# A fused linear attention and feed-forward kernel: token chunks of 512 instead of 384, with the buffers and PSUM banks shared out anew

## The chip, the cores and the metric

The kernel runs on one core of a Trainium2 chip. The metric is the device time of one launch in microseconds (us). A core has TensorE (PE in the profile; its weight loads are PEld), VectorE (DVE), ScalarE (ACT), GpSimd (POOL) and SyncE (SP), which here issues every DMA. PSUM, where PE writes its sums, has eight banks; one bank holds 512 float32 values in each of the 128 partitions.

## The reference

```python
kv  = np.einsum('bhsd,bhse->bhde', k, v)          # 8 batches, 8 heads, 576 positions, 64 wide
out = np.einsum('bhsd,bhde->bhse', q, kv)
rms = np.sqrt(np.mean(out * out, axis=-1, keepdims=True) + 1e-06)
x   = out / rms * g_norm                          # rearranged to 4608 tokens x 512
h   = x @ w_in                                    # 512 x 2048
g   = h * np.cos(h)
y   = g @ w_out                                   # 2048 x 512
```

The two weight matrices come as float64, and the tokens of all batches stand one behind the other.

## The kernel before, in words

The 4608 tokens are cut into 12 chunks of 384 (`CH`). For a chunk, the d_ff dimension of 2048 is walked in 16 blocks of 128 (`j`). One chunk with one block is a *step*, so there are 192 steps. Every float32 operand of a large product is held as a high and a low part, and a product is three matmuls (high x high, low x high, high x low).

A step has these parts. **Stage 1** (`stage1_part`) makes h for the block: for each of 4 slices `p` of the 512 features a triple of matmuls 384 columns wide, 12 in all, into one PSUM bank `ps_h` (three of them, tokens `t_h`). **The elementwise chain** (`act_part`) is, in order: `ki` on ACT (h over 2 pi, rounded), two DVE instructions that reduce h to `r`, sine and square on ACT (half the angle: cos h = 1 - 2 sin² (h/2)), a DVE product with h, which is the last reader of the bank and gives it back, then `ghi` on ACT and `glo` on DVE. **Stage 2** (`stage2_part`) multiplies g by the block of w_out: for each tile of 128 tokens a triple of matmuls 512 columns wide into a bank `acc` that sums over all of d_ff (three tiles and three banks, 9 matmuls). The two banks left, `ps_a`, serve the attention.

Attention for a chunk is done beside the steps of the chunk ahead of it: `kv_part` makes k^T v of a pair of heads, `x_part` turns q into x for one slice `p` (transposes on DVE, the product with kv, the norm with a power on POOL) and writes `xhi` and `xlo`, of which a chunk's tiles are held in a pool of two. The first two chunks (`FRONT`) take another path: PE transposes q and the products are plain float32. `w_part` turns each 128-row block of float64 weights into a high and a low float32 part, with about three instructions on ACT and three on DVE, 512 wide; 32 such halves (16 of w_in, 16 of w_out) are made. So that not all are needed at once, the first steps run as: chunk 0 with blocks 0 to 7, chunk 1 with blocks 0 to 7, chunk 0 with 8 to 15, chunk 1 with 8 to 15, then chunk by chunk. The partial sums of chunks 0 and 1 go to DRAM in between.

The order of instructions on PE, ACT, DVE and POOL is fixed ahead of time by a planner in the kernel (`Order`). Each part is a generator that waits for events, takes tokens (one for each buffer) and asks for time on an engine with a priority; `due(i)` gives the priorities of step `i`. The durations in these requests are written by hand, and the planner's own times decide nothing but the order. SP works through its DMAs in order. At the end `out_part` copies each `acc` bank to SBUF on ACT (buffers `ob`, two of them; the last tile of the last chunk goes into a spare `kt` buffer) and stores it.

```python
    t_x, t_wst, t_h, t_ki, t_r, t_g, t_osb = Tokens(2), Tokens(3), Tokens(3), Tokens(2), Tokens(3), Tokens(3), Tokens(2)
    def due(i):
        return 20.0 + 4.0 * i
    segments = [(0, 0, 8), (1, 0, 8), (0, 8, 16), (1, 8, 16)]
```

Of the kernel before, what the change touches and what calls it, by code (L numbers as in the profile page):

```python
# [19 lines left out]
P = 128  # L20
# [125 lines left out]
def tile_kernel(  # L146
# [16 lines left out]
    CH = 384  # L163
# [19 lines left out]
    ps_h = ctx.enter_context(tc.tile_pool(name="ps_h", bufs=3, space=bass.MemoryType.PSUM))  # L183
# [16 lines left out]
    def copiers(on_act, on_dve):  # L200
        return [("ACT", on_act, 0.0), ("DVE", on_dve, 0.3)]
# [45 lines left out]

    def due(i):
        return 20.0 + 4.0 * i
# [22 lines left out]
    x_slot = [Event() for _ in range(NCH)]  # L272
# [3 lines left out]
    t_kv, t_q, t_qT, t_qhl = Tokens(2), Tokens(2), Tokens(1), Tokens(2)  # L276
    t_s1, t_s2, t_psa = Tokens(4), Tokens(1), Tokens(2)
    t_x, t_wst, t_h, t_ki, t_r, t_g, t_osb = Tokens(2), Tokens(3), Tokens(3), Tokens(2), Tokens(3), Tokens(3), Tokens(2)
# [93 lines left out]
    def kv_part(b, p, prio):  # L372
        yield "wait", [kv_in[b, p]] + ([q_used[c, p] for c in chunks_of(b - 2)] if b > 1 else [])
        yield "take", t_psa, prio
        _, end = yield "run", [("PE", 0.95 if b >= FRONT else 1.1)], prio if b < FRONT else -1.0
# [14 lines left out]
        else:  # L390
            e, end = yield "run", copiers(0.21, 0.27), prio
# [6 lines left out]
        yield "run", [("ACT", 0.21)], prio  # L398
# [6 lines left out]
        _, end = yield "run", [("DVE", 0.27)], prio  # L405
# [9 lines left out]
    def kv_split_part(b, p, prio):  # L415

        yield "wait", [kv_done[b, p]]
        yield "run", [("ACT", 0.18)], prio
# [8 lines left out]
    def x_tiles(c):  # L427
        yield "take", t_x
        _, _ = yield "run", [("NONE", 0.0)], -1.0
        xs[c] = (  # L430
            xpool.tile([P, NP, CH], F32R, name="xhi"),
            xpool.tile([P, NP, CH], F32R, name="xlo"),
        )
        sched.fire(x_slot[c], sched.busy["NONE"])
# [6 lines left out]
    def x_part(c, p, prio):  # L441
        yield "wait", [q_in[c, p], x_slot[c]]
        front = c < FRONT
        yield "take", t_qhl, prio
        if front:
            bank = t_psa if c else t_h
            yield "take", bank, prio
            _, _ = yield "run", [("PE", 0.4)], prio
# [6 lines left out]
        else:  # L455
            yield "take", t_qT
            _, end = yield "run", [("DVE", 0.47)], prio
# [3 lines left out]
        if front:  # L461
            e, end = yield "run", copiers(0.41, 0.47), prio
            qT = at.tile([P, CH], F32, name="qhi")
            copy(e, qT, ps_t[:, 0:CH])
            sched.give(bank, end)
        else:
            yield "run", [("ACT", 0.41)], prio
            qhi = at.tile([P, CH], F32R, name="qhi")
            qlo = at.tile([P, CH], F32R, name="qlo")
# [6 lines left out]
        bank = t_acc[p] if c == 0 and p < NTT else t_psa  # L476
        yield "take", bank, prio
        _, end = yield "run", [("PE", 0.5 if front else 0.5 if len(parts) == 1 else 0.7)], prio if front else -1.0
# [12 lines left out]
        sched.give(t_qhl, end)  # L491
        yield "take", t_s1, prio
        yield "run", [("ACT", 0.37)], prio
        sq = at.tile([P, CH], F32, name="s1", bufs=4)
        act.activation(out=sq, in_=ps[:, 0:CH], func=AF.Square, scale=0.125)
        if front:
            t_xn = t_r if c == 0 and p < NTT else t_s1
            yield "take", t_xn, prio
            _, end = yield "run", [("ACT", 0.46)], prio
            x = ew.tile([P, CH], F32, name="r") if t_xn is t_r else at.tile([P, CH], F32, name="s1", bufs=4)  # L500
            act.activation(out=x, in_=ps[:, 0:CH], func=AF.Copy, scale=gcol)
            _, end = yield "run", [("PE", 0.6)], prio
            sums = ps[:, CH:CH + 2 * NTT]
# [3 lines left out]
            yield "run", [("DVE", 0.13)], prio  # L507
            ms = small.tile([P, 2 * NTT], F32, name="ms")
            dve.tensor_scalar(out=ms, in0=sums, scalar1=EPS, scalar2=None, op0=ALU.add)
            yield "run", [("POOL", 1.2)], prio  # L510
            rinv = small.tile([P, 2 * NTT], F32, name="rinv")
            pool.tensor_tensor(out=rinv, in0=ms, in1=mhalf[:, 0:2 * NTT], op=ALU.pow)
            yield "run", [("ACT", 0.41)], prio
# [10 lines left out]
            sched.give(bank, end)  # L524
        else:
            t_xn = t_s1
            yield "take", t_s2
            yield "run", [("DVE", 0.47)], prio
            sqT = at.tile([P, TB, 32], F32, name="s2", bufs=1)
            dve.transpose(out=sqT.rearrange("p a b -> p (a b)"), in_=sq)  # L530
# [289 lines left out]
```

## Time and profile before

| what | value |
|---|---|
| time, median of 3 runs | 912.48 us (912.03 to 914.66) |
| the profiled execution | 911.69 us, of which the traced span is 909.9 us |
| PE busy | 892.2 us, 98% |
| PE weight loads | 797.2 us, 88% |
| DVE busy | 629.2 us, 69% |
| ACT busy | 553.5 us, 61% |
| POOL busy | 107.6 us, 12% |
| HBM read and written | 46.66 MB and 11.01 MB |

The span is what the trace shows of the program; 1.8 us of the execution's time lie outside it. PE's busy time counts a matmul from its start to its modelled end, and neighbours overlap, so that a PE shown as full can still be waiting a little. What matters for PE is the distance from one matmul's start to the next. The trace has phases: up to about 80 us the DMA engines are full and the weights are made, up to about 150 us the other half of the weights is made, and from then on the steps repeat.

### The profile page before, as it was taken

The page shows a single profiled execution, that of the slowest core. Times are in us where ns is not written, and L with a number is a line of the kernel's source. Part 1 is how long each engine was busy: PE and PEld are TensorE (multiplying, and loading weights), DVE is VectorE, ACT ScalarE, POOL GpSimd, SP SyncE. Part 2 cuts the span into 40 slices and gives each one's busy share as a digit, 9 for nine tenths or more (in the row PEclk, how much of TensorE's full clock was granted, in tenths as well). Part 3 has the DMA queues.
Part 4 walks back from the last instruction along what each step waited for, and adds up shares of the span by engine and source line. Part 5 has one row for each costly group of instructions (what it writes and reads, how often), then busy time and mean ns, then how long its engine had stood idle before and what let it go on. Part 6 is the DMA issues. An engine that isn't in the chain of part 4 may idle for free.

```text
span 909.9 us, 13803 instructions
## 1 busy us (share of the span) xinstructions
PE 892.2 (98%) x5008; PEld 797.2 (88%) x5008; DVE 629.2 (69%) x1276; ACT 553.5 (61%) x1283; POOL 107.6 (12%) x61
## 2 busy tenths in 40 slices
PE   8799998999999999999999999999999999999998
PEld 6787887898899998898889998898889999899997
DVE  3779889877767767767766766776766776766553
ACT  4888887655556555556556656655555665655554
POOL 2120000220101100002000101110110110210000
PEclk9999999999999999999999999999999999999999
DMA  9998010723201003212212002211200110100000
GB/s 247 257 316 282 21 58 2 182 61 88 64 9 52 11 15 91 44 35 70 62 35 53 10 9 79 62 36 52 61 11 10 44 18 9 45 1 1 35 1 35
DMA packets 112244, 58.58 MB, mean 64 GB/s; under 512 B 80432, under 2 KB 103984, under 8 KB 112176
## 3 DMA queue, kind: packets, MB, share of 16 engines
q1 hardware_dynamic: 112176, 57.70, 23.8%
q8 instruction: 39, 0.64, 0.3%
q14 instruction: 29, 0.24, 0.1%
HBM read 46.66 MB, written 11.01 MB: 63 GB/s over the span
## 4 chain that ended last, share of the span: by engine, by line
PE 90%; DMA 3%; DVE 3%; SPq 1%; ACT 1%; issue 1%; POOL 0%; ACTq 0%; DVEq 0%
PE acc L196 43%; PE ps_h L196 42%; PE ps_a L196 5%; DMA wo<-in_moe_w_out_dram 1%; DMA wi<-in_moe_w_in_dram 1%; DVE r L196 1%; DVE sg L196 1%; DMA out_dram<-ob 1%; DMA wo<-in_v_dram 1%; SPq L324 1%; SPq L367 0%; DVE wi L196 0%; DVE glo L196 0%; POOL rinv L196 0%; ACT ki L196 0%
## 5 line engine op out<-in xcount | busy, mean ns | idle before, releaser
L196 PE MATMUL ps_h<-xhi,wi 128*128 128x384 f32 x1536 | 397.1, 339 | 5.6 <-DVE r L196 3.6
L196 PE MATMUL acc<-wo,ghi 128*128 128x512 f32 x1152 | 360.6, 394 | 2.6 <-ACT ghi L196 1.9
L196 PEld LDWEIGHTS ps_h<-xhi,wi 128*128 128x128 f32 x1536 | 281.2, 189 | 22.5 <-DVE r L196 4.8
L196 PE MATMUL ps_h<-xlo,wi 128*128 128x384 f32 x768 | 259.4, 338 | 0.0
L196 ACT ACTIVATE r<-r 128x384 f32<-128x384 f32 x384 | 200.4, 524 | 81.5 <-DVE r L196 76.6
L196 PEld LDWEIGHTS acc<-wo,ghi 128*128 128x128 f32 x1152 | 211.8, 188 | 38.8 <-ACT ghi L196 2.6
L196 PE MATMUL acc<-wo,glo 128*128 128x512 f32 x576 | 227.2, 394 | 0.1
L196 POOL TENSOR_TENSOR rinv<-ms,mhalf 128x12 f32<-128x12 f32 (+1 forms) x48 | 104.8, 2183 | 711.8 <-DVE ms L196 710.6
L196 ACT ACTIVATE ki<-ps_h 128x384 int32<-128x384 f32 x192 | 94.2, 491 | 140.6 <-PE ps_h L196 139.8
L196 DVE SCALAR_TENSOR_TENSOR r<-ki,ps_h 128x384 f32<-128x384 int32 x192 | 105.8, 552 | 87.7 <-ACT ki L196 84.8
L196 DVE SCALAR_TENSOR_TENSOR r<-r,ps_h 128x384 f32<-128x384 f32 x192 | 105.4, 550 | 60.0 <-ACT r L196 59.4
L196 PEld LDWEIGHTS ps_h<-xlo,wi 128*128 128x128 f32 x768 | 144.6, 188 | 0.0
L196 PEld LDWEIGHTS acc<-wo,glo 128*128 128x128 f32 x576 | 108.0, 187 | 24.4 <-DVE glo L196 0.8
L196 DVE TENSOR_TENSOR glo<-r,ghi 128x384 fp32r<-128x384 f32 x192 | 105.7, 551 | 23.9 <-ACT ghi L196 22.3
L196 DVE SCALAR_TENSOR_TENSOR r<-ki,r 128x384 f32<-128x384 int32 x192 | 105.9, 552 | 2.3
L196 ACT CAST ghi<-r 128x384 fp32r<-128x384 f32 x192 | 97.5, 509 | 16.2 <-DVE r L196 14.7
L196 DVE STREAM_TRANSPOSE s<-s 128x384 f32<-128x384 f32 x40 | 23.1, 578 | 41.0 <-ACT s L196 40.7
L196 ACT ACTIVATE s<-ps_a 128x384 f32<-128x384 f32 x45 | 22.1, 491 | 47.1 <-PE ps_a L196 46.9
L196 ACT COPY swp<-part 32x12 f32<-32x12 f32 x160 | 31.7, 198 | 15.8 <-DVE part L196 13.9
L196 DVE STREAM_TRANSPOSE s<-rinv 128x384 f32<-128x384 f32 x40 | 23.0, 575 | 11.2 <-POOL rinv L196 11.1
L196 ACT CAST xhi<-s 128x384 fp32r<-128x384 f32 x45 | 23.0, 511 | 12.1 <-DVE s L196 11.7
L196 DVE TENSOR_TENSOR xlo<-s,xhi 128x384 fp32r<-128x384 f32 x45 | 25.0, 555 | 6.8 <-ACT xhi L196 4.9
(97 smaller groups left out, 517.0 us busy)
## 6 DMA issues: line engine op xcount, KB each, us to landing
out_dram<-ob SPq DMA_DIRECT2D x35, 256.0 KB, 2.1
wi<-in_moe_w_in_dram SPq DMA_DIRECT2D x16, 512.0 KB, 8.5
wo<-in_moe_w_out_dram SPq DMA_DIRECT2D x16, 512.0 KB, 9.1
kt<-in_k_dram SPq DMA_DIRECT2D x24, 256.0 KB, 2.9
vt<-in_v_dram SPq DMA_DIRECT2D x24, 256.0 KB, 3.2
qb<-in_q_dram SPq DMA_DIRECT2D x112, 48.0 KB, 2.3
qb<-in_q_dram SPq DMA_DIRECT2D x96, 24.0 KB, 1.9
part<-ob SPq DMA_DIRECT2D x6, 256.0 KB, 2.0
```

Of the source, the lines that this page charges most:

```text
L196: return lambda *a, **kw: tc.keep_in_program_order(f(*a, **kw))
L324: nc.sync.dma_start(out=t, in_=src[b, 2 * p:2 * p + 2].rearrange("h (p i) d -> p h i d", p=SF))
```

## The change

Chunks are 512 tokens, so there are 9 chunks and 144 steps. A step has 12 matmuls of 512 columns in stage 1 and four tiles, again 12 matmuls, in stage 2. Four banks now hold `acc`, two hold `ps_h`, two `ps_a`. Elementwise instructions are 512 wide. For space, the weight staging shares its buffers (`m`, `sg`, three of each) with the high and low part of q, `ki` has one buffer instead of two, and x is held by slice: six tiles of each kind, four for a chunk and two for the next. Chunk 0 keeps its slices 2 and 3 in the `kt` and `vt` buffers, which are thus taken until step 23; the loads of k and v for batch 2 and later wait for that. The written-in durations and priorities follow (`STEP` is 5.4).

```diff
-    CH = 384
+    CH = 512
-    xpool = ctx.enter_context(tc.tile_pool(name="xpool", bufs=2))
-    wst = ctx.enter_context(tc.tile_pool(name="wst", bufs=3))
+    xpool = ctx.enter_context(tc.tile_pool(name="xpool", bufs=6))
-    at = ctx.enter_context(tc.tile_pool(name="at", bufs=2))
+    at = ctx.enter_context(tc.tile_pool(name="at", bufs=3))
-    ps_h = ctx.enter_context(tc.tile_pool(name="ps_h", bufs=3, space=bass.MemoryType.PSUM))
+    ps_h = ctx.enter_context(tc.tile_pool(name="ps_h", bufs=2, space=bass.MemoryType.PSUM))
+    STEP = 5.4
     def due(i):
-        return 20.0 + 4.0 * i
+        return 20.0 + STEP * i
-    t_s1, t_s2, t_psa = Tokens(4), Tokens(1), Tokens(2)
-    t_x, t_wst, t_h, t_ki, t_r, t_g, t_osb = Tokens(2), Tokens(3), Tokens(3), Tokens(2), Tokens(3), Tokens(3), Tokens(2)
+    t_kv, t_q, t_qT, t_two = Tokens(2), Tokens(2), Tokens(1), Tokens(3)
+    t_s1, t_psa = Tokens(3), Tokens(2)
+    t_x, t_h, t_ki, t_r, t_g, t_osb = Tokens(6), Tokens(2), Tokens(1), Tokens(3), Tokens(3), Tokens(2)
+    def x_tokens(c, p):
+        return t_kv if c == 0 and p >= 2 else t_x
...
-                    out=h, lhsT=w[:, s, cols], rhs=x[:, p, :],
+                    out=h, lhsT=w[:, s, cols], rhs=x,
+            if last_step[c] == i:
+                sched.give(x_tokens(c, p), end)
...
-        prio = due(i + 2) - 4.0
+        prio = due(i + 2) - STEP
-        ki = ew.tile([P, CH], I32, name="ki", bufs=2)
+        ki = ew.tile([P, CH], I32, name="ki", bufs=1)
...
-        first, n = window(chunks_of(b)[0] - 1)
+        first, n = window(chunks_of(b)[0])
-            load(2.1, due(i) - 6.0, [kv_in[b, p]], kv_loads(b, p), take=t_kv)
+            load(2.1, due(i) - 6.0, [kv_in[b, p]], kv_loads(b, p),
+                 wait=[x_done[0, 2], x_done[0, 3]], take=t_kv)
```

Three places in the instruction order follow; tiles have their number behind the name. The first is PE in the steady part, before: the end of one h, a stage 2 of three tiles, and the start of the next h.

```order
L196 MATMUL ps_h_5283<-xhi_3769,wi14_1610 128x384 x2
L196 MATMUL ps_h_5283<-xlo_3770,wi14_1610 128x384
L196 MATMUL acc0_4710<-wo12_1613,ghi_5299 128x512 x2
L196 MATMUL acc0_4710<-wo12_1613,glo_5300 128x512
L196 MATMUL acc1_4717<-wo12_1613,ghi_5299 128x512 x2
L196 MATMUL acc1_4717<-wo12_1613,glo_5300 128x512
L196 MATMUL acc2_4761<-wo12_1613,ghi_5299 128x512 x2
L196 MATMUL acc2_4761<-wo12_1613,glo_5300 128x512
L196 MATMUL ps_h_5283<-xhi_3769,wi14_1610 128x384 x2
L196 MATMUL ps_h_5283<-xlo_3770,wi14_1610 128x384
L196 MATMUL ps_h_5332<-xhi_3769,wi15_1669 128x384 x2
L196 MATMUL ps_h_5332<-xlo_3770,wi15_1669 128x384
```

The same in the changed kernel: the last triple of one h, a stage 2 of four tiles, the first triple of the next h.

```order
L195 MATMUL ps_h_4509<-xhi_4172,wi5_676 128x512 x2
L195 MATMUL ps_h_4509<-xlo_4173,wi5_676 128x512
L195 MATMUL acc0_4352<-wo4_915,ghi_4536 128x512 x2
L195 MATMUL acc0_4352<-wo4_915,glo_4537 128x512
L195 MATMUL acc1_4364<-wo4_915,ghi_4536 128x512 x2
L195 MATMUL acc1_4364<-wo4_915,glo_4537 128x512
L195 MATMUL acc2_4369<-wo4_915,ghi_4536 128x512 x2
L195 MATMUL acc2_4369<-wo4_915,glo_4537 128x512
L195 MATMUL acc3_4375<-wo4_915,ghi_4536 128x512 x2
L195 MATMUL acc3_4375<-wo4_915,glo_4537 128x512
L195 MATMUL ps_h_4582<-xhi_3534,wi6_825 128x512 x2
L195 MATMUL ps_h_4582<-xlo_3535,wi6_825 128x512
```

With two banks, h of step i + 2 goes into the bank of h of step i. Between the end of the one and the start of the other stand, in nearly every step of the changed kernel, the four triples of step i + 1 and four triples of one stage 2. Before, a bank came back three steps later.

The second place is SP's queue where k and v of batch 2 are loaded for the first time, before: among the weight loads.

```order
L367 DMA wi12_795<-in_moe_w_in_dram 128x4x128
L336 DMA qb_944<-in_q_dram 32x12x32 x4
L336 DMA qb_961<-in_q_dram 32x12x32 x4
L313 DMA kt_985<-in_k_dram 128x2x256
L367 DMA wo10_818<-in_moe_w_out_dram 128x512
L313 DMA vt_986<-in_v_dram 128x2x256
L367 DMA wi13_832<-in_moe_w_in_dram 128x4x128
```

And in the changed kernel:

```order
L742 DMA part1_3_1348_1642<-ob_1635 128x512
L723 DMA ob_1944<-part0_0_1000_1158 128x512
L723 DMA ob_2038<-part0_1_1012_1172 128x512
L321 DMA kt_1840<-in_k_dram 128x2x256
L321 DMA vt_1841<-in_v_dram 128x2x256
L321 DMA kt_1866<-in_k_dram 128x2x256
L321 DMA vt_1867<-in_v_dram 128x2x256
L321 DMA kt_1899<-in_k_dram 128x2x256
L321 DMA vt_1900<-in_v_dram 128x2x256
```

The loads moved behind all weights and behind the partial sums, and each waits for the buffer in which chunk 0 kept its slices. On PE, between the last use of the first such buffer (slice 2 of step 23) and the first kv product stand one triple of step 23, two of step 24 and three of a stage 2.

The third place is the end of ACT's queue, before:

```order
L196 CAST ghi_9604<-r_9573 128x384
L196 ACTIVATE r_9607<-r_9607 128x384 x2
L196 CAST ghi_9632<-r_9607 128x384
L196 ACTIVATE ob_9645<-acc0_9144 128x512
L196 ACTIVATE ob_9651<-acc1_9150 128x512
L196 ACTIVATE kt_9653<-acc2_9177 128x512
```

And in the changed kernel:

```order
L195 ACTIVATE r_8154<-r_8154 128x512 x2
L195 CAST ghi_8178<-r_8154 128x512
L195 ACTIVATE ob_8188<-acc0_7653 128x512
L195 ACTIVATE ob_8193<-acc1_7658 128x512
L195 ACTIVATE kt_8200<-acc3_7667 128x512
L195 ACTIVATE ob_8203<-acc2_7662 128x512
```

There is a fourth tile to store; its copy comes last, and uses an `ob` buffer that the first tile's store must have left.

## Rows read from the trace of the kernel before

**Rows 1.** The page's busy times of PE, DVE and ACT over the span.

```profile
PE 892.2 (98%) x5008; PEld 797.2 (88%) x5008; DVE 629.2 (69%) x1276; ACT 553.5 (61%) x1283; POOL 107.6 (12%) x61
```

**Rows 2.** The chain that ended last, shares of the span by line.

```profile
PE acc L196 43%; PE ps_h L196 42%; PE ps_a L196 5%; DMA wo<-in_moe_w_out_dram 1%; DMA wi<-in_moe_w_in_dram 1%; DVE r L196 1%; DVE sg L196 1%; DMA out_dram<-ob 1%; DMA wo<-in_v_dram 1%; SPq L324 1%; SPq L367 0%; DVE wi L196 0%; DVE glo L196 0%; POOL rinv L196 0%; ACT ki L196 0%
```

**Rows 3.** Windows: PE, PEld, DVE, ACT, POOL busy (count), granted clock, DMA share, GB/s.

```profile
40.00:77.00 37.00, 32.43 (x207) 28.10 (x207) 32.27 (x64) 33.30 (x75) 6.29 (x4) 0.95 0.98 299
77.00:112.60 35.60, 35.55 (x177) 32.10 (x178) 30.91 (x62) 29.02 (x61) 0.00 (x0) 1.00 0.37 125
112.60:148.30 35.70, 32.63 (x160) 28.27 (x159) 30.75 (x57) 28.74 (x58) 0.00 (x0) 1.00 0.12 37
200.00:880.00 680.00, 679.16 (x3733) 612.04 (x3732) 461.31 (x943) 393.87 (x928) 82.61 (x36) 1.00 0.15 38
```

**Rows 4.** Instructions grouped by form, up to 76.9 us: count, busy us, mean ns.

```profile
L196 PE MATMUL ps_h<-xhi,wi 128*128 128x384 f32 x64 | 19.7, 388 | 2.3 <-DVE r L196 1.7 <-DVE wi L196 0.6
...
L196 PE MATMUL acc<-wo,ghi 128*128 128x512 f32 x30 | 9.9, 412 | 0.4 <-ACT ghi L196 0.4
```

**Rows 5.** The same groups up to 112.6 us.

```profile
L196 PE MATMUL ps_h<-xhi,wi 128*128 128x384 f32 x128 | 36.1, 363 | 3.8 <-DVE r L196 3.3 <-DVE wi L196 0.6
L196 PE MATMUL acc<-wo,ghi 128*128 128x512 f32 x84 | 26.7, 399 | 0.4 <-ACT ghi L196 0.4
```

**Rows 6.** The same groups up to 148.3 us.

```profile
L196 PE MATMUL ps_h<-xhi,wi 128*128 128x384 f32 x192 | 52.8, 355 | 5.2 <-DVE r L196 3.3 <-ACT wi L196 1.1 <-DVE wi L196 0.8
L196 PE MATMUL acc<-wo,ghi 128*128 128x512 f32 x126 | 39.9, 398 | 1.9 <-ACT ghi L196 1.9
```

**Rows 7.** The last links of the chain in order of time: start us, us.

```profile
891.84 2.10 PE ps_h L196 x12
893.94 2.08 PE acc L196 x9
...
898.13 8.22 PE acc L196 x36
...
906.37 0.60 ACT kt L196
```

**Rows 8.** Elementwise groups by form over the whole span, 384 and 512 wide.

```profile
L196 ACT ACTIVATE r<-r 128x384 f32<-128x384 f32 x384 | 200.4, 524 | 81.5 <-DVE r L196 76.6
...
L196 DVE SCALAR_TENSOR_TENSOR r<-r,ps_h 128x384 f32<-128x384 f32 x192 | 105.4, 550 | 60.0 <-ACT r L196 59.4
...
L196 ACT ACTIVATE ki<-ps_h 128x384 int32<-128x384 f32 x192 | 94.2, 491 | 140.6 <-PE ps_h L196 139.8
...
L196 DVE SCALAR_TENSOR_TENSOR sg<-sg,m 128x512 int32<-128x512 int32 x32 | 21.9, 686 | 2.7 <-ACT m L196 2.1 <-ACT sg L196 0.6
L196 ACT ACTIVATE ob<-acc 128x512 f32<-128x512 f32 x35 | 20.9, 596 | 9.1 <-PE acc L196 4.7 <-DMA out_dram<-ob 4.0
```

**Rows 9.** Timeline of ACT and DVE after an h that ended at 893.94 us.

```profile
893.98 0.49 ACT L196 ACTIVATE ki<-ps_h 128x384 int32<-128x384 f32 x1 [1.05 <-PE ps_h L196]
...
894.50 0.56 DVE L196 SCALAR_TENSOR_TENSOR r<-ki,ps_h 128x384 f32<-128x384 int32 x1 [0.99 <-ACT ki L196]
...
894.98 0.55 DVE L196 TENSOR_TENSOR glo<-r,ghi 128x384 fp32r<-128x384 f32 x1
...
895.45 0.55 DVE L196 SCALAR_TENSOR_TENSOR r<-ki,r 128x384 f32<-128x384 int32 x1
...
897.14 0.55 DVE L196 SCALAR_TENSOR_TENSOR r<-r,ps_h 128x384 f32<-128x384 f32 x1 [1.15 <-ACT r L196]
```

**Rows 10.** Waits from 200 to 880 us: PE's for a bank of h.

```profile
PEld ps_h L196 <- DVE r L196: 0.4, 1, 0.4
```

**Rows 11.** DMA issues: count, KB each, median us to landing.

```profile
kt<-in_k_dram SPq DMA_DIRECT2D x24, 256.0 KB, 2.9
vt<-in_v_dram SPq DMA_DIRECT2D x24, 256.0 KB, 3.2
```

More of the change, by code (lines that the diff above doesn't have):

```diff
@@ L390, in kv_part @@
         else:
-            e, end = yield "run", copiers(0.21, 0.27), prio
+            e, end = yield "run", [("ACT", 0.41, 0.0), ("DVE", 0.45, 0.3)], prio
             for j in range(2):
@@ L397, in kv_part @@
             return
-        yield "run", [("ACT", 0.21)], prio
+        yield "run", [("ACT", 0.41)], prio
         his = []
@@ L404, in kv_part @@
             his.append(hi)
-        _, end = yield "run", [("DVE", 0.27)], prio
+        _, end = yield "run", [("DVE", 0.44)], prio
         for j in range(2):
@@ L456, in x_part @@
             yield "take", t_qT
-            _, end = yield "run", [("DVE", 0.47)], prio
+            _, end = yield "run", [("DVE", dve_us())], prio
             qT = at.tile([P, CH], F32, name="qT", bufs=1)
@@ L461, in x_part @@
         if front:
-            e, end = yield "run", copiers(0.41, 0.47), prio
-            qT = at.tile([P, CH], F32, name="qhi")
+            e, end = yield "run", copiers(), prio
+            qT = at.tile([P, CH], F32, name="m")
             copy(e, qT, ps_t[:, 0:CH])
@@ L475, in x_part @@
         yield "wait", [kv_done[b, p] if front or b >= FRONT else kv_split[b, p] for b, _, _, _ in parts]
-        bank = t_acc[p] if c == 0 and p < NTT else t_psa
+        bank = t_acc[p] if c == 0 else t_psa
         yield "take", bank, prio
-        _, end = yield "run", [("PE", 0.5 if front else 0.5 if len(parts) == 1 else 0.7)], prio if front else -1.0
+        pe_us = sum(0.88 * n / 512 if front else 3 * max(0.11, (n + 32) / 2400) for _, _, _, n in parts)
+        _, end = yield "run", [("PE", pe_us)], prio if front else -1.0
         ps = ps_o.tile([P, DM], F32, name=f"acc{p}") if bank is not t_psa else ps_tile(t_psa)
@@ L521, in x_part @@
             sched.give(t_s1, end)
-            _, end = yield "run", [("DVE", 0.47)], prio
+            _, end = yield "run", [("DVE", dve_us())], prio
             dve.tensor_tensor(out=x, in0=x, in1=ps[:, 0:CH], op=ALU.mult)
@@ L534, in x_part @@
             sched.give(t_s1, end)
-            sched.give(t_s2, end)
-            yield "run", [("ACT", 0.41)], prio
+            sched.give(t_qT, end)
+            yield "run", [("ACT", 0.8)], prio
             swp = small.tile([P, TB], F32, name="swp")
@@ L546, in x_part @@
             yield "take", t_s1, prio
-            yield "run", [("DVE", 0.47)], prio
-            x = at.tile([P, CH], F32, name="s1", bufs=4)
+            yield "run", [("DVE", dve_us())], prio
+            x = at.tile([P, CH], F32, name="s1")
             dve.transpose(
@@ L714, in out_part @@
             yield "wait", [come]
-            _, end = yield "run", [("DVE", 0.6)], prio
+            _, end = yield "run", [("DVE", dve_us(DM))], prio
             dve.scalar_tensor_tensor(out=o, in0=acc, scalar=-2.0, in1=o, op0=ALU.mult, op1=ALU.add)
         else:
-            _, end = yield "run", [("ACT", 0.48)], prio
+            _, end = yield "run", [("ACT", act_us(DM))], prio
             if spare:
@@ L756, in tile_kernel @@
                 sched.spawn(g_part())
-    for c in range(NCH):
-        sched.spawn(x_tiles(c))
     for c in range(FRONT):
```

123 lines of the change are left out of this document (61 added, 62 removed).

## The prediction

> **What bounds the kernel now.** I read the shares of the span first, then the chain, then the stretches. PE is busy 98% of the span, DVE 69%, ACT 61% [rows 1]; since busy time of PE says little about its pace, the chain decides: stage 2 (`acc`) holds 43% of it, stage 1 (`ps_h`) 42%, the attention's `ps_a` 5% [rows 2]. In the steady part, from 200 to 880 us, PE is busy in 679.16 of 680 us at full granted clock [rows 3]. There the only thing that can help is less PE time.
>
> The beginning is different. Up to 76.9 us PE has done 64 of the high stage-1 matmuls (8 in a step: 8 steps) and 30 of the high stage-2 ones (6 in a step: 5 steps) [rows 4]. A stage 1 takes 2.10 us and a stage 2 takes 2.08 us when PE runs through [rows 7]; together these make 8 x 2.10 + 5 x 2.08 = 27.2 us, and the rest of the 76.9 is attention and waiting. From 40 to 77 us DVE is busy 32.27 and ACT 33.30 of 37 us [rows 3], so both elementwise engines are close to full there. From 77 to 112.6 us the counts grow by 64 and 54 [rows 4, 5], 8 and 9 steps, or 16.8 + 18.7 = 35.5 of 35.6 us: PE is packed. From 112.6 to 148.3 us they grow by 64 and 42 [rows 5, 6], 8 and 7 steps, 16.8 + 14.6 = 31.4 of 35.7 us. So 4.3 us are lost in the second batch of weights, while DVE is busy 30.75 of 35.7 us, 86% [rows 3], and PE's first matmuls wait for `r`, `wi` and `ghi` [rows 6].
>
> **Stage 1, wider matmuls.** 192 x 12 matmuls of 384 columns become 144 x 12 of 512. At 384, twelve take 2.10 us, 175 ns each. At 512 the trace has stage 2: nine in 2.08 us, 231 ns each, or 36 in 8.22 us, 228 ns each [rows 7]. I take 231, which stands in the mixed stretch as the 175 does: a stage 1 of 12 x 0.231 = 2.77 us. Then 192 x 2.10 = 403.2 us become 144 x 2.77 = 398.9 us: 4.3 us less. The bounds: at 228 ns it is 144 x 2.74 = 394.6, 8.6 us less; if the time only grows with the columns (175 x 4/3 = 233 ns), nothing. Stage 2 keeps its 1728 matmuls and its time, three tiles in 192 steps against four in 144.
>
> The Trainium skill ("TensorE: Matmul & The Clock Gate", section Back-to-back issue gap) gives an isolated gap of N / 2.4 + 2.5 ns when warm, 162.5 and 215.8 ns here. By it stage 1 would fall from 374.4 to 372.9 us, 1.5 us, and the sum below would be 905.3. The trace does not agree on the size: both widths take some 12 to 15 ns more than that.
>
> **The second batch of weights, 77 to 148 us.** The halves to be made stay as they are; a step's four DVE instructions in the chain grow by 686 - 550 = 136 ns each [rows 8], 8 x 4 x 0.136 = 4.4 us in 8 steps, while PE's 8 steps grow to 8 x 5.54 = 44.3 us. DVE then has 30.75 + 4.4 = 35.2 us to do in 44.3, 79% instead of 86%. I take all 4.3 us of PE's loss as regained; bounds 0 and 4.3.
>
> **The first batch, up to 77 us.** DVE and ACT set the pace. In the order, 47 of DVE's instructions ahead of the end of the 16th weight half are 384 wide; at 136 ns more they take 6.4 us more, and step 8 starts that much later. But PE has then done 8 steps of stage 1 and 5 of stage 2 that are each larger: 8 x (2.77 - 2.10) + 5 x (2.77 - 2.08) = 8.8 us of work that is not to be done later. Net gain 2.4 us. Bounds: 8.8 if the wider instructions fit in gaps; a loss of 2.5 if ACT's growth (47 x (596 - 491) ns = 4.9 us [rows 8]) comes on top of DVE's. The plain float32 products for 1024 instead of 768 tokens lie in PE's waiting time of this phase; if that were gone they would cost some 2 us, an estimate from the ratio of tokens and the front's share of `ps_a`.
>
> **Two banks for h.** The bank of h comes back after `ki`, two reductions, sine, square and the product. After the h that ended at 893.94 us the product ended at 897.14 + 0.55 [rows 7, 9], 3.75 us later, with one `glo` of another step in between. At 512, four DVE instructions (136 ns more) and three on ACT (105 ns more) make it 4.6 us. The next use of the bank comes 8 triples later, 8 x 0.69 = 5.5 us. So 0.9 us are to spare, one foreign DVE instruction; I take 0. Queued behind a late product on DVE are the next reductions, and for the bank PE waits, with stage 2 behind it in its queue.
>
> **Loads of k and v for batch 2** are free to start when slice 2 of step 23 is done, and have 6 triples, 4.1 us, until the first kv product. They land 2.9 and 3.2 us after issue [rows 11]. I take 0; the bound is their whole 3.2 us, once.
>
> **The end.** Before, the last sum was ready at 898.13 + 8.22 = 906.35 us, its copy ended at 906.97 and its store at 909.9, 2.93 us later [rows 7]. Now the copy that stands last needs the buffer of tile 0: copy 0.62, store 2.93, copy 0.60, store 2.93 make 7.1 us after tile 0's sum, that is 7.1 - 3 x 0.69 = 5.0 us after the last sum instead of 3.55: 1.5 us more (bound 0).
>
> Attention in the steady part moves nothing: x is made for as many tokens, the k and v products are the same, and DVE, busy 461 of 680 us [rows 3], takes fewer and longer instructions. Its cover is PE's packed time; were DVE short there, it would show as the bank's wait.
>
> **Sum.** The profiled execution took 911.7 us (span 909.9 and 1.8 around it), 0.8 below the median of the runs, 912.48. 911.7 - 4.3 - 4.3 - 2.4 + 1.5 = 902.2; with a little of the 0.8 added, 902.5 us.
>
> **Rivals.**
> *The banks of h bind (slower).* Place: every step after the front, about 112. For it: only 0.9 us of slack, and x's DVE instructions (one 512 wide costs 0.69 us) stand between chain links; two in a row use it up. Against it: with three banks PE waited for a bank 0.4 us once from 200 to 880 us [rows 10], and between second reduction and product DVE is idle while ACT does sine and square (1.15 us [rows 9]), where one such instruction fits. It decides at 7 us / 112 = 0.06 us per step; at 0.15 us the time is 902.5 + 17 = 919. The skill ("Perfetto Trace Analysis", section Optimization Strategy) has it that a gap that repeats on the engine that should be full can mean too little PSUM for the next tile; by that rule this is what the trace would show. Chance 0.13.
> *The front gives nothing back.* Staging shared by weights and x (three sets for both, five before) or ACT's share makes the first phase lose 2.5 us, and the second stall stays: 902.5 + 4.9 + 4.3 = 911.7, no change. For it: ACT and DVE both near 90% up to 77 us. Chance 0.14.
> *More comes back.* The wide instructions fit into the first phase's gaps (8.8 instead of 2.4) and matmuls run at 228 ns: 902.5 - 6.4 - 4.3 = 891.8. For it: before, PE waited for data there as well as for engines. Chance 0.13.
> *As forecast*, 897 to 908: chance 0.60.
>
> **Numbers.** 0.3% of the time, 2.7 us, is about what a measurement of this kernel can tell from no change. Faster by more than that: forecast and "more", 0.73; the same: 0.14; slower: 0.13. The range 893 to 912 holds the forecast, the case without gain in the front and half of "more", about 0.8.
>
> **What would show it.** Right: in the steady part PE packed, with twelve `ps_h` matmuls in 2.77 us; 8 steps in the second batch of weights without waits of PE for `wi` or `ghi`; step 8 starting at 82 to 86 us; about 5 us from the last sum to the end. Wrong: a row of PE or its weight loads waiting for `r` that counts dozens of times (the banks); a step 8 near 90 us; PE waiting for `kt`; `ps_h` matmuls of 512 columns that take more than 233 ns.

## The result, and the profile after

The changed kernel takes 918.86 us, median of 4 runs (917.98 to 920.62), against 913.06 (912.03 to 914.66) for the kernel before: a ratio of 1.0064, 95% interval 1.0042 to 1.0087. It is 0.6% slower, and outside the range that was forecast. Its profiled execution took 920.62 us with a span of 918.7, 8.8 us more than the profiled execution of the kernel before (the medians differ by 5.8 us).

The page's busy times of the changed kernel answer to [rows 1]:

```profile
PE 886.2 (96%) x4464; PEld 719.3 (78%) x4464; DVE 597.6 (65%) x997; ACT 518.7 (56%) x1000; POOL 100.4 (11%) x49
```

PE has less to do than before, as forecast (886.2 us instead of 892.2), and the span is longer all the same. So there is more waiting, and the windows say where; they are those of [rows 3], with the columns as there, of the changed kernel:

```profile
40.00:77.00 37.00, 29.61 (x167) 24.14 (x167) 23.82 (x43) 23.78 (x50) 1.64 (x1) 0.86 1.01 275
77.00:112.60 35.60, 29.61 (x130) 23.58 (x129) 27.45 (x49) 25.42 (x45) 5.71 (x3) 0.86 0.38 115
112.60:148.30 35.70, 34.84 (x153) 28.19 (x152) 32.77 (x55) 31.47 (x58) 0.00 (x0) 1.00 0.08 30
200.00:880.00 680.00, 676.18 (x3380) 550.70 (x3380) 444.00 (x739) 368.86 (x728) 83.01 (x28) 1.00 0.17 45
```

From 40 to 77 us DVE is busy 23.82 us where it was 32.27, and ACT 23.78 instead of 33.30: the engines that the forecast took to be too full have become emptier. PE is emptier too, in both of the first windows, and its granted clock is 0.86 of full speed there, a mean over stretches at either level. From 112.6 us on PE is packed again.

The last links of the chain, which answer to [rows 7] (start us, us):

```profile
893.97 2.72 PE ps_h L195 x12
896.69 2.72 PE acc L195 x12
906.21 6.14 PE acc L195 x27
```

Twelve matmuls of 512 columns take 2.72 us in both stages, 227 ns each. The run that ends at 912.35 us is not the last sum but that of the first of four tiles; what follows is on ACT (timeline; start, us, in brackets the idle time before and its releaser):

```profile
914.42 0.60 ACT L195 ACTIVATE kt<-acc 128x512 f32<-128x512 f32 x1 [0.76 <-PE acc L195]
915.16 0.60 ACT L195 ACTIVATE ob<-acc 128x512 f32<-128x512 f32 x1
```

The fourth tile's sum was ready at 914.39 us (its last matmul began at 914.00 and took 0.39), so the end took 918.7 - 914.39 = 4.3 us instead of 3.55.

The 8.8 us can now be divided. Step 8, the first step of chunk 1, begins at 108.71 us; before, at 77.05. That is 31.7 us later. From there to the last sum it is 805.7 us, where it was 906.35 - 77.05 = 829.3: 23.6 us less. The end is 0.75 us longer. 31.7 - 23.6 + 0.75 = 8.8. **All of the loss arose ahead of step 8, and afterwards the change gave more than was forecast.**

What is late there? Step 8 needs x of chunk 1. In the kernel before, the transposes of the first slice of q of chunk 1 on PE, the last of its low parts on DVE and step 8 stand here (rows of the timelines of PE and DVE):

```profile
31.18 0.49 PE L196 MATMUL ps_a<-ident,wo 128*128 128x128 f32 x3
...
77.05 0.62 PE L196 MATMUL ps_h<-xhi,wi 128*128 128x384 f32 x2 [1.58 <-DVE r L196]
```

```profile
70.31 0.55 DVE L196 TENSOR_TENSOR xlo<-s,xhi 128x384 fp32r<-128x384 f32 x1
```

In the changed kernel, the four k-v products of chunk 1, the first transposes of its q, and step 8 on PE, and the four low parts on DVE:

```profile
34.11 0.92 PE L195 MATMUL ps_a<-wi,wo 96*64 96x64 f32 x24 [1.62 <-DMA wi<-in_v_dram]
38.87 0.92 PE L195 MATMUL ps_a<-wo,wi 96*64 96x64 f32 x24 [1.86 <-DMA wo<-in_v_dram]
45.31 1.55 PE L195 MATMUL ps_a<-wo,wi 96*64 96x64 f32 x24 [3.93 <-DMA wo<-in_v_dram]
50.32 1.55 PE L195 MATMUL ps_a<-wo,wo 96*64 96x64 f32 x24 [3.47 <-DMA wo<-in_v_dram]
...
65.77 1.03 PE L195 MATMUL ps_a<-ident,wo 128*128 128x128 f32 x8
...
108.71 0.62 PE L195 MATMUL ps_h<-xhi,wi 128*128 128x512 f32 x2
```

```profile
80.02 0.69 DVE L195 TENSOR_TENSOR xlo<-s,xhi 128x512 fp32r<-128x512 f32 x1
87.92 0.69 DVE L195 TENSOR_TENSOR xlo<-s,xhi 128x512 fp32r<-128x512 f32 x1
95.92 0.69 DVE L195 TENSOR_TENSOR xlo<-s,xhi 128x512 fp32r<-128x512 f32 x1
100.71 0.68 DVE L195 TENSOR_TENSOR xlo<-s,xhi 128x512 fp32r<-128x512 f32 x1
```

Two things stand out. The k-v products wait for their loads, and the steps behind them in PE's queue wait with them (10.9 us in the four rows). And x of chunk 1 starts 34.6 us later than before (65.77 against 31.18) and is ready 30.4 us later (100.71 against 70.31), about what step 8 lost. The last transposes of its norm and step 7, in PE's queue behind them, stand here:

```profile
98.20 0.66 PE L195 MATMUL ps_a<-ident,s 128*128 128x128 f32 x4 [3.10 <-DVE m L195]
100.24 1.22 PE L195 MATMUL ps_h<-xhi,wi 128*128 128x512 f32 x2 [1.38 <-DVE r L195]
```

Here, too, work waits for work that stands ahead of it in the queue: step 7 stands behind the transposes, which wait 3.10 us, and then waits 1.38 us itself for a bank. PE's waits for v up to 109 us are, in all (us, times, longest):

```profile
PE ps_a L195 <- DMA wo<-in_v_dram: 9.3, 3, 3.9
...
PE ps_a L195 <- DMA wi<-in_v_dram: 4.7, 3, 2.0
```

### The profile page after: what moved, and what is told of

It reads as the page before. It is cut to its first block, busy times and chain, and to the rows that moved or that the text cites. A ratio compares the mean times of both kernels' runs of the same rounds, so it can differ in the third digit from the quotient of the medians.

```text
span 918.7 us, 12050 instructions
## 1 busy us (share of the span) xinstructions
PE 886.2 (96%) x4464; PEld 719.3 (78%) x4464; DVE 597.6 (65%) x997; ACT 518.7 (56%) x1000; POOL 100.4 (11%) x49
## 4 chain that ended last, share of the span: by engine, by line
PE 85%; DMA 5%; DVE 4%; ACT 2%; SPq 1%; POOL 1%; issue 1%; POOLq 0%; DVEq 0%; ACTq 0%
PE acc L195 40%; PE ps_h L195 39%; PE ps_a L195 6%; DMA wo<-in_moe_w_out_dram 2%; DVE r L195 2%; POOL rinv L195 1%; DMA wo<-in_v_dram 1%; DMA wi<-in_moe_w_in_dram 1%; SPq L332 1%; DVE s L195 0%; ACT s L195 0%; DVE glo L195 0%; SPq L359 0%; POOLq L826 0%; ACT ki L195 0%
## 5 line engine op out<-in xcount | busy, mean ns | idle before, releaser
L195 PE MATMUL ps_h<-xhi,wi 128*128 128x512 f32 x1088 | 343.5, 397 | 6.0 <-DVE r L195 6.0
L195 ACT ACTIVATE r<-r 128x512 f32<-128x512 f32 x288 | 181.9, 631 | 106.7 <-DVE r L195 102.4
L195 PE MATMUL ps_h<-xlo,wi 128*128 128x512 f32 x544 | 213.2, 392 | 0.0
L195 POOL TENSOR_TENSOR rinv<-ms,mhalf 128x16 f32<-128x16 f32 (+1 forms) x36 | 97.6, 2712 | 697.9 <-DVE ms L195 691.4
L195 DVE SCALAR_TENSOR_TENSOR r<-r,ps_h 128x512 f32<-128x512 f32 x144 | 98.6, 684 | 99.7 <-ACT r L195 99.2
L195 DVE SCALAR_TENSOR_TENSOR r<-ki,ps_h 128x512 f32<-128x512 int32 x144 | 98.5, 684 | 80.9 <-ACT ki L195 80.4
L195 ACT ACTIVATE ki<-ps_h 128x512 int32<-128x512 f32 x144 | 86.0, 597 | 98.4 <-PE ps_h L195 97.2
L195 ACT CAST ghi<-r 128x512 fp32r<-128x512 f32 x144 | 89.0, 618 | 53.7 <-DVE r L195 53.2
L195 DVE TENSOR_TENSOR glo<-r,ghi 128x512 fp32r<-128x512 f32 x144 | 98.1, 682 | 32.5 <-ACT ghi L195 31.7
L195 DVE SCALAR_TENSOR_TENSOR r<-ki,r 128x512 f32<-128x512 int32 x144 | 98.9, 687 | 2.1
L195 DVE STREAM_TRANSPOSE qT<-s 128x512 f32<-128x512 f32 x28 | 19.9, 712 | 30.2 <-ACT s L195 30.1
```

What stands on the lines that cost most here:

```text
L195: return lambda *a, **kw: tc.keep_in_program_order(f(*a, **kw))
```

## The experiments

Three theories were open at first. **A**: the four k-v products stand in PE's queue ahead of work that is ready, and their loads are late. **B**: the elementwise engines, or the staging buffers that feed them, set the pace of the first 100 us. **C**: the two banks of h cost there, not in the steady part.

**The k-v products behind steps 2 to 5.**

```diff
+    def gated_kv(c, p, part):
+        if c:
+            yield "wait", [gates[2 + p]]
+        yield from part
-            sched.spawn(kv_part(c, p, t))
+            sched.spawn(gated_kv(c, p, kv_part(c, p, t)))
```

> Changed kernel, but the four k-v products of the second chunk may be ordered on PE only after steps 2 to 5 have begun, one each. Theory A (the front lost its time because these products stand ahead of step 2 in PE's queue while their loads have not landed): PE's waits for the loads of v up to step 8 fall from 14 us to under 5, step 8 starts at 85 to 95 us instead of 108.7, and the time falls by 12 to 22 us, to 898 to 909. Theory B (ACT, DVE and the three shared staging buffers set the pace of the front): step 8 stays later than 104 us and the time changes by less than 4 us. Theory C (the two banks of h cost the time, all along): the time changes by less than 4 us.

Measured: 911.03 us (909.67 to 915.42), ratio to before 0.9987 (0.9966 to 1.0009). PE's waits for v fell to 2.2 us, in two rows, and step 8 came at 97.8 instead of 108.7. But new waits of the same stretch took the place of some (PE's waits up to 109 us: us in total, times, longest):

```profile
PE ps_h L195 <- DVE r L195: 9.1, 3, 5.5
...
PE ps_a L195 <- DMA wi<-in_v_dram: 2.2, 2, 1.2
```

That is some 8 us less than the changed kernel and level with the kernel before: in the direction of A, and less than A expected (step 8 by 95 us, 898 to 909). Moving four products also moves everything that the planner places behind them, so the run doesn't say yet what the cause is.

**The same loads dearer, or earlier.** In one kernel the planner reckons with DMAs 1.3 times as long, so that it places what needs them later; in the other the loads of chunk 1 go earlier into SP's queue.

```diff
-            _, end = yield "run", [("DMA", us)], prio
+            _, end = yield "run", [("DMA", 1.3 * us)], prio
```

> Changed kernel with the planner's transfer times 1.3 times as long, so that the order it writes expects the loads about when the trace shows them; nothing else is changed. Theory A: the order now fits the loads, PE's waits for v fall below 7 us in sum, step 8 starts before 98 us and the time falls by 8 to 22 us. Theory B: less than 4 us. Theory C: less than 4 us.

Measured: 917.46 us (911.68 to 923.38), ratio 1.0045 (1.0015 to 1.0075). Step 8 came at 98.7 us, 10 us earlier; from there to the last sum it took 814.2 us instead of 805.7, in an order that is another everywhere, so that most of it was given back.

```diff
-            t = due(begin[c]) - 28 + 3 * p if c else -100.0 + p
+            t = due(begin[c]) - 40 + 3 * p if c else -100.0 + p
```

> Changed kernel, but the loads of k, v and q of the second chunk have the priorities that they had in absolute time before the change (12 us earlier), so they stand further ahead in SP's queue, and their products further ahead on PE. Theory A: the loads land earlier, PE waits less for them (under 9 us instead of 14), but weights of steps 2 to 4 land later; the time falls by 3 to 10 us. Theory B: no change within 4 us, or slower since the weights come later.

Measured: 915.25 us, ratio 1.0028 (1.0010 to 1.0046), step 8 at 103.5. PE's waits for v fell from 14.0 us to 7.1, and the time by some 3.6, within what A expected. So less waiting for v is worth something, but half of the waiting gave back only 5.2 of the 31.7 us that step 8 lost.

**Banks.** The kernel before with two banks of h instead of three, everything else kept:

```diff
-    ps_h = ctx.enter_context(tc.tile_pool(name="ps_h", bufs=3, space=bass.MemoryType.PSUM))
+    ps_h = ctx.enter_context(tc.tile_pool(name="ps_h", bufs=2, space=bass.MemoryType.PSUM))
```

> Kernel before (chunks of 384) with two banks for h instead of three, all else kept. Theory C (two banks are what costs): slower than before by over 8 us, PE waiting for r of an earlier step dozens of times after 200 us. Theory A or B: under 5 us slower, since a bank at 384 is needed again after about 4.2 us, while the chain needs 3.4 us at least; the price in the steady part of the changed kernel was about 4 us.

Measured: 937.67 us (936.11 to 938.70), ratio 1.0275 (1.0242 to 1.0308). At 384 columns the third bank is worth 25 us: step 8 at 86.5 instead of 77.0, and from 200 to 920 us PE's weight loads wait for a bank again and again (us in total, times, longest):

```profile
PEld ps_h L196 <- DVE r L196: 21.4, 43, 2.0
```

In the changed kernel, from 200 to 880 us, it is half as often, and PE itself (second row) waited seven times:

```profile
PEld ps_h L195 <- DVE r L195: 11.0, 21, 1.7
```

```profile
PE ps_h L195 <- DVE r L195: 3.7, 7, 1.3
```

With wider steps two banks cost less, though not nothing (the price is worked out below). Giving the changed kernel a third bank, at the price of one of the attention's two, brings nothing:

```diff
-... name="ps_h", bufs=2, ...      t_h = Tokens(2)      name="ps_a", bufs=2, ...      t_psa = Tokens(2)
+... name="ps_h", bufs=3, ...      t_h = Tokens(3)      name="ps_a", bufs=1, ...      t_psa = Tokens(1)
```

> Changed kernel with three banks for h and one for the attention instead of two and two; nothing else. Theory C2 (with two banks h of a step waits, in the front, for a chain that stands between weight instructions, and the rest of the front follows): step 8 starts 8 us or more earlier than in the changed kernel (108.7), PE's waits for r fall below 5 us in sum, the time falls by 8 to 20 us. Theory A (late loads of k and v ahead in PE's queue are the only cause): PE's waits for v stay at about 14 us and the time changes by less than 4 us, or rises if one attention bank is too few.

Measured: 921.13 us, ratio 1.0090 (1.0066 to 1.0115). PE now waits for a bank of h three times from 112 to 880 us, 4.5 us in all, and once 5.2 us at the attention's one bank; step 8 came at 106.6, and the last low part of x of chunk 1 at 111.8, even behind it. PE's waits for v fell to 2.6 us here, which by A should have helped, and the time did not fall. If C gave anything, the attention's one bank took it back. The same with the k-v products moved behind steps 2 to 5 as well:

> The first experiment's late k-v products and three banks for h with one for the attention, together. If both causes hold side by side: the front reaches step 8 at about 85 us and the time is 893 to 903. If the banks do nothing once the products are late (A alone): 908 to 913, as with late products alone. If one attention bank is a new limit: slower than late products alone, with PE or ACT waiting on the attention's tiles after 200 us.

Measured: 924.15 us, ratio 1.0121 (1.0100 to 1.0143). That is some 13 us more than with the late products alone, the third of the expected cases: one attention bank is a limit of its own. So these two do not support C, and they cannot rule it out; a kernel with three banks and two for the attention would need a ninth bank and was not tried.

**The other buffer that was taken away.** `ki` has one buffer in the change; here it has two, and `qb` two instead of three to make room.

```diff
-        ki = ew.tile([P, CH], I32, name="ki", bufs=1)
+        ki = ew.tile([P, CH], I32, name="ki", bufs=2)
```

> Changed kernel with two buffers for ki again instead of one (room for it from a q buffer that no token used); nothing else. Theories A and C2: no change within 4 us, since ki is read by the two reductions that follow it. A rival (the single ki buffer holds up the next step's chain): 4 us or more faster, with ACT's waits at ki shorter.

Measured: 919.80 us, ratio 1.0080 (1.0052 to 1.0108), no change clear of the noise. With three banks of h and the late products it is the same:

> Three banks for h, one for the attention, late k-v products and two buffers for ki, all together. If the causes add: as with three banks and late products, or up to 5 us faster; step 8 at about 83 us, 890 to 902 us in all.

Measured: 921.19 us, ratio 1.0092 (1.0070 to 1.0114).

**The staging, undone and done alone.** This leaves B. In the change three staging sets (`m`, `sg`) serve the weight halves and the q of every slice, where there were three sets for the weights and two for q. Two kernels test it from both sides. The first is the changed kernel in which the q of the first two chunks goes into buffers that lie idle then:

```diff
-        yield "take", t_two, prio
+        t_own = t_two if not front else t_qT if c else t_g
+        yield "take", t_own, prio
...
-            qT = at.tile([P, CH], F32, name="m")
+            qT = at.tile([P, CH], F32, name="qT", bufs=1) if c else ew.tile([P, CH], F32, name="ghi")
...
-        sched.give(t_two, end)
+        sched.give(t_own, end)
```

> The changed kernel with one edit: in the front the transposed q of chunk 0 goes into a ghi buffer and that of chunk 1 into the qT buffer, which both lie idle then, so that the three staging sets serve the weights alone. Theory A (the k-v products of chunk 1, whose loads come late, stand in PE's queue ahead of work that is ready): those products still stand there, step 8 starts within 3 us of 108.7, time 915 to 920. Theory B (the shared staging holds the weight halves up): step 8 starts by 100 us and the time falls to 911 or less.

Measured: **905.74 us** (904.00 to 908.25), ratio 0.9926 (0.9903 to 0.9948), 13.1 us less than the changed kernel and faster than the kernel before, with two banks of h as in the change. Step 8 comes at 92.7. The k-v products were not touched, and yet PE's waits for v fell from 14.0 to 3.9 us. How that goes together is seen in PE's order (- the changed kernel, + this one; `64x64` are k-v products, `ident` transposes of q, `qT` the product with kv):

```
 L195 MATMUL acc_333<-ident,s_344 128x128 x4
+L195 MATMUL ps_a<-ident,wo_379 128x128 x4
 L195 MATMUL ps_h<-kt,wi_228 128x512 x2
 L195 MATMUL ps_h<-vt,wi_228 128x512
 L195 MATMUL ps_h<-kt,wi_375 128x512 x2
 L195 MATMUL ps_h<-vt,wi_375 128x512
+L195 MATMUL ps_a<-qT,wo_138 128x64
+L195 MATMUL ps_a<-qT,wo_138 128x448
 L195 MATMUL ps_a<-wo_411,wi_410 64x64 x12
...
-L195 MATMUL ps_a<-wo_475,wi_474 64x64 x12
-L195 MATMUL ps_a<-wo_525,wo_524 64x64 x12
+L195 MATMUL ps_a<-pair,s_498 128x2 x4
+L195 MATMUL ps_a<-ident,wo_379 128x128 x4
 L195 MATMUL ps_h<-xhi,wi_433 128x512 x2
```

In the changed kernel no slice of chunk 1 can begin while weight halves hold the three sets. The two `ps_a` banks are therefore free, and the planner fills them with the next k-v products, one after the other, whose loads are not there yet. With buffers of its own, q takes a bank in between, and the third and fourth product come later by themselves. So A's wait is real, but in this order it follows from B. The timelines of this kernel, PE (first transposes of the slices, step 8) and DVE (first and last low part):

```profile
36.38 1.06 PE L195 MATMUL ps_a<-ident,wo 128*128 128x128 f32 x4
...
44.35 1.08 PE L195 MATMUL ps_a<-ident,wo 128*128 128x128 f32 x4
...
92.69 0.73 PE L195 MATMUL ps_h<-xhi,wi 128*128 128x512 f32 x2
```

```profile
69.42 0.69 DVE L195 TENSOR_TENSOR xlo<-s,xhi 128x512 fp32r<-128x512 f32 x1
...
91.35 0.68 DVE L195 TENSOR_TENSOR xlo<-s,xhi 128x512 fp32r<-128x512 f32 x1
```

The first transposes are back from 65.77 to 36.38 us, and step 8 starts 0.7 us after the last low part ends. In the window from 40 to 60 us DVE is busy 17.66 us (first row, this kernel), where the changed kernel had 11.71 (second):

```profile
40.00:60.00 20.00, 17.07 (x90) 13.62 (x89) 17.66 (x30) 16.67 (x33) 0.00 (x0) 0.83 1.10 308
```

```profile
40.00:60.00 20.00, 12.61 (x83) 10.24 (x83) 11.71 (x20) 12.52 (x29) 0.00 (x0) 0.74 1.09 296
```

The windows up to step 8 show what came back: the kernel before, the changed kernel, and this one.

```profile
0.00:77.05 77.05, 66.99 (x481) 56.40 (x482) 51.83 (x103) 56.85 (x128) 15.46 (x21) 0.98 1.03 274
0.00:108.71 108.71, 85.20 (x540) 66.70 (x541) 66.43 (x122) 68.06 (x131) 17.43 (x21) 0.86 0.85 226
0.00:92.69 92.69, 81.84 (x541) 64.56 (x541) 61.79 (x113) 67.09 (x131) 17.86 (x21) 0.91 0.98 260
```

PE stood idle for 10.1 us ahead of step 8 in the kernel before, for 23.5 in the changed kernel, and for 10.9 here. So nearly all of the added waiting is gone. The rest of the later step 8 is PE's own work: it is busy for 81.8 us instead of 67.0.

The weights show the other half of the sharing. In the changed kernel the low parts of the tenth and the eleventh weight half are made on DVE at:

```profile
65.74 0.69 DVE L195 TENSOR_TENSOR wo<-sg,wo 128x512 fp32r<-128x512 f32 x1 [1.50 <-ACT wo L195]
78.73 0.69 DVE L195 TENSOR_TENSOR wi<-sg,wi 128x512 fp32r<-128x512 f32 x1
```

and with q's own buffers at:

```profile
61.47 0.69 DVE L195 TENSOR_TENSOR wo<-sg,wo 128x512 fp32r<-128x512 f32 x1 [1.40 <-ACT wo L195]
68.19 0.68 DVE L195 TENSOR_TENSOR wi<-sg,wi 128x512 fp32r<-128x512 f32 x1
```

By the priorities in the code, ten halves (up to 41.0) go ahead of the four slices of chunk 1 (43.2 to 46.2), and the eleventh, which step 6 needs, goes behind them (46.4). So q waits for ten halves, and then the weights wait for q: 13.0 us between the two low parts, and 6.7 with buffers of its own; before, it was 7.9. In the ten kernels with 512 columns and shared staging the gap is 13 to 26 us, and in the four with q's own buffers 7 to 8. With the late k-v products it is 20.0 us, and there x of chunk 1 was ready at 93.5 us, hardly later than here (92.0): step 8 came 4.3 us after it, behind a wait of 2.88 us for a bank, so x alone did not keep it back.

From the other side, the kernel before, with chunks of 384 and all banks as they were, and a sharing of the staging:

```diff
+    t_wst = t_qhl
...
-            qT = at.tile([P, CH], F32, name="qhi")
+            qT = wst.tile([P, DM], F32, name="m")[:, 0:CH]
...
-            qhi = at.tile([P, CH], F32R, name="qhi")
-            qlo = at.tile([P, CH], F32R, name="qlo")
+            qhi = wst.tile([P, DM], F32R, name="m")[:, 0:CH]
+            qlo = wst.tile([P, DM], F32R, name="sg")[:, 0:CH]
```

> The kernel before with one part of the change alone: three staging sets shared by the weights and by q, where it had three for the weights and two for q. Theory A: no dearer than 3 us, 912 to 916, step 8 at 77 to 80. Theory B: the front loses what the change lost and did not get back with the late products, 5 us or more, 917 or above, step 8 at 82 or later.

Measured: 950.41 us (949.59 to 951.83), ratio 1.0415 (1.0389 to 1.0441), 38 us dearer. The sign that was named for it failed: step 8 begins at 77.0 us, as in the kernel before, because the first slice of x was ready. But after the first triples of three steps no further triple of stage 1 comes until 119.4. PE's timeline, then ACT's:

```profile
86.50 0.49 PE L196 MATMUL ps_a<-ident,wo 128*128 128x128 f32 x3
107.15 1.65 PE L196 MATMUL ps_a<-m,wo 128*128 128x192 f32 x4 [20.16 <-ACT m L196]
```

```profile
81.92 0.66 ACT L196 ACTIVATE m<-wo 128x512 int32<-128x512 uint32 x1
...
105.56 0.66 ACT L196 ACTIVATE m<-wo 128x512 int32<-128x512 uint32 x1
106.63 0.47 ACT L196 COPY m<-ps_a 128x384 f32<-128x384 f32 x1
```

q of a slice was transposed at 86.5 us, and its copy into `m` came 20 us later, behind weight copies into the same buffers (eight on ACT from 81.92 to 105.56, seven of them after the transposes), while PE stood still. The stall is another than in the changed kernel, and so is the order: in the change the weights ask for a set with a priority (`yield "take", t_two, prio`), and here, as in the kernel before, without one, which the planner serves first. So here q stands behind the weights of the second batch too (the sixteenth half is done at 80.9 us, 82.7 in the kernel before), and in the change ahead of the eleventh half. The run shows that sharing can cost this much by its order; it does not size the sharing of the change.

**What adds to it.** With q's own buffers, the k-v products late, and the last two tiles stored from the two `kt` buffers:

```diff
-        spare = c == NCH - 1 and t == NTT - 1
+        spare = c == NCH - 1 and t >= NTT - 2
```

> All that may help together: k-v products of chunk 1 behind steps 2 to 5, own buffers for q in the front, and the last two tiles stored from the two kt buffers. Theory A with the end term: 911.0 as with the late products alone, less 2 to 3 us for the end, 908 to 909. Theory B adds what the staging gives in the stretch from 60 to 80 us, where with the late products alone DMA and DVE were both under full: 900 to 906.

Measured: 906.97 us (904.88 to 908.54), ratio 0.9937 (0.9916 to 0.9958), no better than q's own buffers alone; step 8 at 95.7. Once the staging is free, moving the products brings nothing. This and the next expectation also misread the end: the 6.35 us in them run from the first tile's sum, as shown above.

> The k-v products of chunk 1 behind steps 2 to 5, and the last two tiles stored from the two kt buffers, so that the copy of the last one waits for no store. If the end was the second copy's wait, the span ends 3.6 us or a little more after the last sum instead of 6.35, and the time is 2 to 3 us less than with the late products alone: 908 to 909. If the stores themselves are late, it stays at 911.

Measured: 911.52 us (909.09 to 913.92), ratio 0.9984 (0.9967 to 1.0001). The end took 909.7 - 906.13 = 3.57 us instead of 4.3, which is too little to show in the time.

**What holds x of chunk 1 from there?** With q's own buffers it is still ready at 92 us only. Each slice takes two of three `s1` buffers (before, of four); here its x goes into a `qb` buffer that is idle until chunk 2.

```diff
-            t_xn = t_r if c == 0 else t_s1
+            t_xn = t_r if c == 0 else t_q
```

> q of the front in buffers of its own, and x of chunk 1 in an idle qb buffer, so that a slice takes one s1 buffer instead of two; the loads of q for chunk 2 wait until x of chunk 1 is done. If the three s1 buffers pace x of chunk 1: its last low part ends by 87 us instead of 92, step 8 starts by 88 us, and the time is 900 to 903. If DVE and ACT pace it: step 8 at 91 to 94 and the time 904 to 907, as with q's own buffers alone.

Measured: **903.93 us** (903.66 to 905.84), ratio 0.9909 (0.9890 to 0.9928); step 8 at 90.3, the last low part from 88.95. Between the two expectations, 1.8 us below q's own buffers alone and within their spread. In both kernels PE is busy without a gap from 52 us to step 8, so x was no longer what PE waited for there. The same with both spare buffers at the end:

> The same with the last two tiles stored from the two kt buffers. Its instructions up to the end are the same, so only the end differs: 2.8 us less from the last sum to the span's end (3.6 instead of 6.4), and 2 to 3 us less in time than the kernel beside it.

Measured: 904.07 us (902.39 to 907.31), ratio 0.9912 (0.9889 to 0.9934): no difference. The last links of the chain of the kernel with one spare buffer, and of this one:

```profile
889.51 6.13 PE acc L195 x27
```

```profile
890.15 8.21 PE acc L195 x36
```

The span of both is 901.9 us. The first row ends with the first tile's sum, and 3 x 0.68 us later, at 897.68, the last is ready, so 4.2 us are left; the second ends with the last sum at 898.36, and 3.5 us are left. The second spare buffer is worth 0.7 us, not the expected 2.8. Last, the changed kernel with the staging shared and only x of chunk 1 in `qb`:

> The changed kernel with the staging still shared, x of chunk 1 in an idle qb buffer. If the shared staging is what holds x of chunk 1 back: its first transposes still come at about 65 us and step 8 at 103 us or later, time 913 to 920. If the s1 buffers were: step 8 by 95 us, 905 to 908.

Measured: 916.71 us (915.24 to 917.18), ratio 1.0039 (1.0021 to 1.0056). The first transposes still come at 65.1 us and step 8 at 105.0. x of chunk 1 was ready at 95.1 us, 6 us earlier than in the changed kernel, and step 8 gained 3.7. So the shared staging holds the front back with `s1` relieved as well. `s1` may cost some 2 us, with the sharing or without, but neither pair of intervals lies apart.

## Why the prediction was wrong

**The step that failed is the first batch, up to 77 us.** It had DVE and ACT set the pace there, priced the wider instructions at 6.4 us, and put step 8 at 82 to 86 us. Step 8 came at 108.7. Neither engine set the pace: both became emptier. What was missed is the sharing of the staging, which that sum didn't price at all; a rival named it in passing and gave it, together with ACT's share, a loss of 2.5 us. Undoing it in the first two chunks took 13.1 us off the time and 12.7 us off PE's waits ahead of step 8. It works through the order: four slices of chunk 1 wait until ten weight halves are done, and the weight halves of steps 6 and 7 wait until those slices give their sets back. That this costs 13.1 us is shown by the run; the two halves of the way there are read from the code and the rows, and no run took them apart. The order of the changed kernel shows it without a time: all four k-v products of chunk 1 stand on PE ahead of the first transpose of its q. The three places that the forecast looked at were others.

A second fault of the same sum shows with the staging apart. It let PE do 8.8 us more work ahead of step 8 and yet put step 8 only 6.4 us later, so PE's waits there had to shrink. They did not (10.9 us against 10.1), and step 8 came at 92.7.

The other terms, one by one. *Stage 1*: the right mechanism, and too small; twelve matmuls take 2.72 us where nothing waits, not 2.77, so 144 x (2.10 x 192 / 144 - 2.72) = 11.5 us less than before instead of 4.3. Stage 2 gained too, 227 ns a matmul instead of 231, which the sum did not have. *Second batch of weights*: more than half as forecast; the 16 steps from step 8 to step 24 took 71.4 us before and 88.9 now, where the two stages take 66.9 and 87.0, so the loss fell from 4.5 to 1.8 us. Step 24 begins here, before and after:

```profile
148.45 0.61 PE L196 MATMUL ps_h<-xhi,wi 128*128 128x384 f32 x2 [0.30 <-DVE r L196]
```

```profile
197.56 0.61 PE L195 MATMUL ps_h<-xhi,wi 128*128 128x512 f32 x2
```

*Two banks at nothing*: not quite. PE's own waits for a bank are 3.7 us in the steady part, but its weight loads wait 11.0, and a matmul that starts late need not show as idle time. From step 24 to the last sum the kernel before took 757.9 us, of which its stages (168 of stage 1, 171 of stage 2) account for 708.5; the changed kernel took 716.8, of which 242 times 2.72 us account for 658.2. Beside the stages there are thus 58.6 us instead of 49.4. The 9.2 us more are an estimate of what the banks cost at most, 0.08 us a step, where the rival took 0.15. That the measured 919 us is also that rival's time is a coincidence: the loss arose ahead of step 8. *Loads of k and v for batch 2*: nothing, as taken; no row of PE between 112 and 300 us waits for them. *The end*: 0.75 us more instead of 1.5.

So after step 8 the change gave 23.6 us, where the sum had 8.8 + 4.3 + 4.3 = 17.4; ahead of it, it lost 31.7 instead of 6.4. The 23.6 can be put together: at full pace the stages from step 8 on are 30.1 us shorter (184 x 2.10 + 187 x 2.08 = 775.4 us before, 274 x 2.72 = 745.3 now); the second batch adds 2.7, and the 9.2 above go off. With the staging apart the time is 905.7, and 903.9 with `s1` relieved. That this is next to the forecast's 902.5 is in part luck: step 8 is still later than forecast there (90.3 us), and the faster matmuls make up for it.

What stays open: how much of the 13.1 us is the weights that wait for q, and how much is q that waits for the weights; and why PE is busy for 14.9 us more ahead of step 8 with the staging apart. The larger steps, 8 of stage 1 and 6 instead of 5 of stage 2, account for 10.9 of them; attention for more tokens and the lower clock (0.91 against 0.98) are left for the rest, and were not taken apart. Four sets shared by both were not tried.

## What to carry to other kernels

When two streams that had buffers of their own share a pool, price it by who stands behind whom in the order, not by the busy time of the engines that fill it: each waits for what stands ahead of it, here q for ten weight halves and the next halves for q, and everything that needs their results waits too. A planner turns such a shortage into another order, and the stall then appears on an unrelated line, here as a wait for v. A theory that removes the visible wait and gets only part of the time back should be tested against the one that explains why the wait is there. And a test that tries one part of a change in the old kernel must bring its order along: here the sharing, tried without the weights' priority, stalled at another place and cost another amount.

## What the hardware showed unexpectedly

Matmuls that all have 512 columns start 227 ns apart, where those of stage 2, mixed with 384, stood 228 to 231 ns apart before [rows 7].

PE's clock was lower where PE waited more. The granted clock from 40 to 77 us was 0.95 before [rows 3] and is 0.86 here. From 45.0 to 55.2 us the records of the changed kernel show the lower level, 1.2 GHz (0.50 in that window), after the waits of 1.86 and 3.93 us in the rows above: 24 k-v matmuls took 1.55 us at 45.31, and 0.92 at 38.87.

The same instructions on two chips began step 8 at 97.8 and 99.0 us (k-v products late, without and with the second spare buffer; the order on PE, DVE and ACT is the same up to the last copy). So a microsecond or two in the front is not to be read from one trace.
